# Keys in runs of 64 KB: one key buffer and two value buffers in the place of a ring of three

## The chip, the core and the metric

The kernel runs on one core of one Trainium2 chip. The metric is the device time of an execution in microseconds: the median of three runs before the change is 189.44 us (189.35 to 189.58). Beside it stands one profiled execution; its span of 187.4 us is the time inside the program that the trace shows. "Same" means within 2%.

## What is computed

One decoding step of a transformer block in its parallel form, for two sequences (B = 2) with one new token each. The normalized row goes through attention over the last W = 4096 positions of a cache and through a dense layer with the mish activation; both are added to the input.

```python
def reference(A_x, A_k_cache, A_v_cache, A_wq, A_wo, B_x, B_w1, B_b1, B_w2):
    # A_x: 2 x 1 x 448; caches: 2 x 8 heads x 32768 x 256; 16 query heads of 256, all bf16
    xn = _layernorm(A_x)
    # attention, W = 4096
    q = (xn @ wq)                             # 16 heads; two of them share a key/value head
    k, v = k_cache[:, :, Sk - W:], v_cache[:, :, Sk - W:]
    scores = einsum("bhqd,bhkd->bhqk", q, k) * 256 ** -0.5
    o = einsum("bhqk,bhkd->bhqd", softmax(scores), v)
    attention = o @ wo
    # dense layer
    h = xn @ w1 + b1
    dense = (h * tanh(softplus(h))) @ w2
    return A_x + attention + dense            # B_x takes no part
```

(Shortened, with the same names.) The keys that are read have 2 x 8 x 4096 x 256 x 2 B = 33.6 MB, the values as much; with the weights wq, wo, w1 and w2 the kernel reads 77.67 MB for each step and computes little with every byte.

## The kernel before

The 16 pairs of sequence and key head are worked through in U = 4 units of J = 4 pairs. The keys of one unit are 8 MiB: each of the 128 partitions takes 128 positions of one pair, 64 KB that lie together in the cache. SBUF is shared out in pools. Keys, values, wq, w1 and w2 go through one ring of three buffers of 32 KB for each partition, so a unit's keys come in two transfers of 4 MiB whose runs are 32 KB long, and its values in two of 4 MiB.

```python
kv_pool = ctx.enter_context(tc.tile_pool(name="kv", bufs=3))
kt_pool = ctx.enter_context(tc.tile_pool(name="kt", bufs=1))
wo_pool = ctx.enter_context(tc.tile_pool(name="wo", bufs=2))
...
KE = T * Dh                                   # 32 * 256; RK = 2

def ring(name):
    return kv_pool.tile([P, RK * KE], BF16, tag="kv", name=name)

def load_k(u, r):
    t = ring("k")
    src = kview[u][:, s0:, :].rearrange("j (c t) d -> c j (t d)", c=C)
    nc.sync.dma_start(out=t[:], in_=src[:, :, r * RK * KE : (r + 1) * RK * KE])
    k_t[u, r] = t

def load_v(u, g, lo=0, hi=TV):
    if lo == 0:
        v_t[u, g] = ring("v")
    ...
```

The waits follow from the buffers: a transfer into a buffer of the ring is issued when the last reader of what the buffer held is done. All the large transfers are issued in program order from the sync queue.

For the scores the keys must lie with the head dimension on the partitions. VectorE transposes them in blocks of 32 x 32, as pairs of bf16 in one fp32, two instructions for each half of a unit's keys; the result of each half has a tile of its own (32 KB for each partition, `kt0` and `kt1`). TensorE multiplies them with the query, ScalarE takes the exponential, VectorE transposes the weights back, and TensorE multiplies them with the values.

```python
kt = [kt_pool.tile([P, T * NB, RK, P // (R * J), J], FP32, name=f"kt{i}") for i in range(NH)]

def turns(u, i):
    t = k_t.pop((u, i))
    for r in range(RK):
        nc.vector.transpose(out=kt[i][:, :, r, :, :], in_=...)      # 128 x 4096 fp32

def scores(u, i):                              # cut
    ...                                        # mask: one matmul with ident
    for n in range(NB):
        for e in range(2):
            for w in range(4):                 # 4 * 2 * 4 = 32 matmuls
                nc.tensor.matmul(sc[32 * w : 32 * (w + 1)]...,
                    lhsT=qd[:, u, 2 * n + e, :, :]..., rhs=ktm[i][:, n, e, :, 16 * w : 16 * (w + 1)], ...)
    nc.scalar.activation(out=ex[:, :, :, i, :], in_=sc[:], func=ACT.Exp, scale=scale)
    if i == NH - 1:
        ...                                    # VectorE: ex transposed to the weights p, swap
```

`weigh` sums the weights, `values` multiplies them with the values, `gather` and `finish` make the unit's output, `relay` and `mix_early` multiply it with wo. The program order, which each engine follows for its own instructions:

```python
load_w1()
turns(0, 0); project(); scores(0, 0); turns(0, 1); dense_in(); mish(); scores(0, 1); weigh(0)
for u in range(U - 1):
    load_k(u + 1, 0); load_v(u, 0); load_k(u + 1, 1); load_v(u, 1); load_wo(u)
    turns(u + 1, 0)
    values(u, 0)
    scores(u + 1, 0)
    turns(u + 1, 1)
    values(u, 1)
    gather(u); finish(u)
    scores(u + 1, 1)
    relay(u); mix_early(u)
    if u < U - 2:
        weigh(u + 1)
u = U - 1
load_v(u, 0); load_v(u, 1, 0, 32); load_wo(u); load_v(u, 1, 32, 56); load_v(u, 1, 56, TV)
for part in range(len(w2_parts)):
    load_w2(part)                              # four transfers, into a buffer of the ring
carry(); values(u, 0); values(u, 1, 32); weigh(u); gather(u, last=False)
values_fixed(u, 1, 32, 56); values_fixed(u, 1, 56, TV); finish(u)
mix(u)                                         # wo of the last unit
for part in range(len(w2_parts)):
    dense_out(part)                            # w2; then the result is stored
```

(Several calls are put on one line here.)

Of the kernel before, what the change touches and what calls it, by code (L numbers as in the profile page):

```python
# [11 lines left out]
BF16 = mybir.dt.bfloat16  # L12
FP32 = mybir.dt.float32
# [4 lines left out]
def kernel(  # L18
# [13 lines left out]
    nc = tc.nc  # L32
    P = 128
    G = 4
    J = 4
    R = 4
    RK = 2

    Bsz, Sq, D = A_x.shape
# [11 lines left out]
    T = CT // R  # L51
# [17 lines left out]

    lead_pool = ctx.enter_context(tc.tile_pool(name="lead", bufs=1))  # L70
    lead_pool.tile([P, 192], BF16, name="lead")
    kv_pool = ctx.enter_context(tc.tile_pool(name="kv", bufs=3))
    kt_pool = ctx.enter_context(tc.tile_pool(name="kt", bufs=1))
    wo_pool = ctx.enter_context(tc.tile_pool(name="wo", bufs=2))
    p_pool = ctx.enter_context(tc.tile_pool(name="pp", bufs=1))
    consts = ctx.enter_context(tc.tile_pool(name="consts", bufs=1))
# [11 lines left out]
    vview = A_v_cache.rearrange("b (k u) s d -> u (b k) s d", u=U)  # L88

    def ring(name):  # L90
        return kv_pool.tile([P, RK * KE], BF16, tag="kv", name=name)

    k_t, v_t, wo_t = {}, {}, {}

    def load_k(u, r):
        t = ring("k")
        src = kview[u][:, s0:, :].rearrange("j (c t) d -> c j (t d)", c=C)
        nc.sync.dma_start(out=t[:], in_=src[:, :, r * RK * KE : (r + 1) * RK * KE])  # L98
        k_t[u, r] = t

    def load_v(u, g, lo=0, hi=TV):
        if lo == 0:
            v_t[u, g] = ring("v")
        t = v_t[u, g]
        src = vview[u][:, s0:, :].rearrange("j (g x t) d -> g x j (t d)", g=GV, x=C)
        nc.sync.dma_start(
            out=t[:, lo * Dh : hi * Dh], in_=src[g, :, :, lo * Dh : hi * Dh]
        )
# [15 lines left out]

    x_bf = consts.tile([Bsz, D], BF16)
    nc.scalar.dma_start(out=x_bf[:, :], in_=A_x.flatten_outer_dims())
    b1_sb = consts.tile([2, F2], BF16)
    nc.scalar.dma_start(out=b1_sb[:], in_=B_b1.rearrange("(k f) -> k f", k=2))

    load_k(0, 0)  # L130
    wq = ring("wq")
    nc.sync.dma_start(  # L132
        out=wq[:, 0 : NS * HW], in_=A_wq.flatten().rearrange("(p e) -> p e", p=P)
    )
    wq_t = [wq[:, i * HW : (i + 1) * HW] for i in range(NS)]
    load_k(0, 1)

    ident = consts.tile([P, P], BF16)
    make_identity(nc, ident[:])
# [12 lines left out]
    for k in range(KU):  # L152
# [14 lines left out]
        out=rstd[:], in_=mv[:, 1:2], func=ACT.Sqrt, bias=eps_t[:], scale=1.0  # L167
    )
    nc.vector.reciprocal(out=rstd[:], in_=rstd[:])
    xn_bf = consts.tile([Bsz, D], BF16)  # L170
    nc.vector.tensor_scalar(
        out=xn_bf[:],
        in0=x_bf[:],
        scalar1=mv[:, 0:1],
        scalar2=rstd[:],
# [31 lines left out]
                )  # L207

    xr_ps = ps_m.tile([P, NS, Bsz], BF16, tag="m", name="xr_ps")
    xn_v = xn_bf[:].rearrange("b (a k) -> b a k", k=NS)  # L210
    for s in range(NS):
        r = s // 2
        step = 3 + s % 2
# [39 lines left out]
    def add_rows(lhsT, rows, stop=False):  # L253
# [7 lines left out]
                skip_group_check=True,  # L261
            )

    kt = [
        kt_pool.tile([P, T * NB, RK, P // (R * J), J], FP32, name=f"kt{i}") for i in range(NH)
    ]
    ktm = [
        kt[i][:].bitcast(BF16).rearrange("p (t n) r c (j e) -> p n e t (r c j)", n=NB, e=2)
        for i in range(NH)
    ]  # L270

    def turns(u, i):
        t = k_t.pop((u, i))
        for r in range(RK):
            nc.vector.transpose(  # L275
                out=kt[i][:, :, r, :, :],
                in_=t[:, r * KE : (r + 1) * KE].bitcast(FP32).rearrange(
                    "p (a c j) -> p a c j", c=P // (R * J), j=J
                ),
            )  # L280

    spread = {}
    for n in range(2):
        for e in range(2):
            o = n * 64 + e
            sp = consts.tile([P, G, 32], BF16, name=f"sp{n}{e}")
            nc.gpsimd.tensor_copy(
                out=sp[:],
                in_=ident[:, o : o + 63 : 2].unsqueeze(1).to_broadcast([P, G, 32]),
            )  # L290
            spread[n, e] = sp

    def project():
        q_ps = ps_m.tile([P, 512], FP32, tag="m", name="q_ps")
        for s in range(NS):
            for u in range(U):
                nc.tensor.matmul(  # L297
                    q_ps[32 * u : 32 * (u + 1), :],
                    lhsT=xs[:, s, :],
                    rhs=wq_t[s][:, u * 512 : (u + 1) * 512],  # L300
                    start=(s == 0),
                    stop=(s == NS - 1),
                    skip_group_check=True,
                )
        q_sb = small.tile([P, 4, P], BF16, tag="vs", name="q_sb", bufs=1)
        nc.scalar.copy(out=q_sb[:].rearrange("p a m -> p (a m)"), in_=q_ps[:])
        qt_ps = ps_m.tile([P, 4, P], BF16, tag="m", name="qt_ps")
        for a in range(4):
            nc.tensor.transpose(qt_ps[:, a, :], q_sb[:, a, :], ident[:])  # L309
        qT = consts.tile([P, 2, U, Bsz, KU, rep], BF16)  # L310
        q_v = qt_ps[:].rearrange("p (h c) (u r) -> p c u r h", c=2, u=U)
        for c in range(2):
            for b in range(Bsz):
                nc.vector.tensor_copy(  # L314
                    out=qT[:, c, :, b, :, :], in_=q_v[:, c, :, b : KU * Bsz : Bsz, :]
                )
        qr_ps = ps_m.tile([P, 2 * NB, U, NQ], FP32, tag="m", name="qr_ps")
        for n in range(NB):
            for e in range(2):
                nc.tensor.matmul(  # L320
                    qr_ps[:, 2 * n + e, :, :].rearrange("p u q -> p (u q)"),
                    lhsT=spread[n % 2, e][:].rearrange("p g a -> p (g a)"),
                    rhs=qT[:, n // 2].rearrange("p u b k h -> p (u b k h)"),
                    start=True,
                    stop=True,
                    skip_group_check=True,
                )
        for g in range(G):
            rows = slice(g * 32, (g + 1) * 32)
            nc.vector.tensor_copy(  # L330
                out=qd[rows, :, :, g, :],
                in_=qr_ps[rows].rearrange("p n u q -> p u n q"),
            )
# [12 lines left out]
    def scores(u, i):  # L346
        if i == 0:
            state["ex"] = small.tile([P, T, 4, NH, J], BF16, tag="ex", name="ex", bufs=1)
        ex = state["ex"]
        sc = ps_sc.tile([P, T, 4, J], FP32, tag="sc", name="sc")  # L350
        nc.tensor.matmul(  # L351
            sc[:].rearrange("p t c m -> p (t c m)"),
            lhsT=ident[:],
            rhs=mneg[:].rearrange("p a j -> p (a j)"),
            start=True,
            stop=False,
            skip_group_check=True,
        )
        for n in range(NB):
            for e in range(2):  # L360
                for w in range(4):
                    nc.tensor.matmul(  # L362
                        sc[32 * w : 32 * (w + 1)].rearrange("p t c m -> p t (c m)"),
                        lhsT=qd[:, u, 2 * n + e, :, :].rearrange("p g q -> p (g q)"),
                        rhs=ktm[i][:, n, e, :, 16 * w : 16 * (w + 1)],
                        start=False,
                        stop=(n == NB - 1 and e == 1),
                        skip_group_check=True,
                    )
        nc.scalar.activation(out=ex[:, :, :, i, :], in_=sc[:], func=ACT.Exp, scale=scale)  # L370
        if i == NH - 1:
            for h in range(NH):
                nc.vector.transpose(  # L373
                    out=p_all[:, :, h * TH : (h + 1) * TH, :].rearrange("p g t q -> p t g q"),
                    in_=ex[:, h * TH : (h + 1) * TH].rearrange(
                        "p t c i m -> p t (c i m)"
                    ).rearrange("p t (g q) -> p t g q", g=G),
                )
            swap()
# [124 lines left out]
    def load_w1():  # L504
        t = ring("w1")
        nc.sync.dma_start(
            out=t[:, 0 : NS * F2], in_=B_w1.flatten().rearrange("(p e) -> p e", p=P)
        )
        state["w1"] = t
# [44 lines left out]

    def load_w2(part):
        if part == 0:
            state["w2"] = ring("w2")
        k, lo, hi = w2_parts[part]
        w2_in = B_w2.flatten().rearrange("(k p e) -> k p e", k=2, p=P)
        at = k * KH  # L560
        nc.sync.dma_start(  # L561
            out=state["w2"][:, at + lo * D : at + hi * D],
            in_=w2_in[k, :, lo * D : hi * D],
        )
# [7 lines left out]
            )  # L572

    load_w1()
    turns(0, 0)
    project()
    scores(0, 0)
# [2 lines left out]
    mish()  # L580
    scores(0, 1)
    weigh(0)
    for u in range(U - 1):
        load_k(u + 1, 0)
        load_v(u, 0)
        load_k(u + 1, 1)
        load_v(u, 1)
        load_wo(u)
        turns(u + 1, 0)
        values(u, 0)  # L590
        scores(u + 1, 0)
        turns(u + 1, 1)
        values(u, 1)
        gather(u)
        finish(u)
        scores(u + 1, 1)
        relay(u)
        mix_early(u)
        if u < U - 2:
            weigh(u + 1)  # L600
    u = U - 1
    load_v(u, 0)
    load_v(u, 1, 0, 32)
    load_wo(u)
    load_v(u, 1, 32, 56)
# [54 lines left out]
```

## Time and profile before

| what | value |
|---|---|
| time, median of 3 runs | 189.44 us |
| span of the profiled execution | 187.4 us |
| read from HBM | 77.67 MB, 414 GB/s over the span |
| VectorE busy | 92.9 us (50%) |
| of it the 16 transposes of keys | 70.1 us, 4417 ns each |
| TensorE busy, matmuls | 78.0 us (42%) |
| ScalarE busy | 12.4 us (7%) |
| GpSimd busy | 4.7 us (2%) |
| mean granted TensorE clock | 0.727 |

How to read it: busy time is the sum of an engine's instructions, and engines work beside each other, so the shares do not add up to 100%. The page cuts the span into 40 slices of 187.4 / 40 = 4.7 us and gives each a digit, the busy share in tenths; 9 is 90% or more. Transfers are counted apart, by queue and by packet. A line of a timeline has the start, the busy time, the engine, the line of the kernel, the operation with its operands and shapes, and in brackets how long the engine had stood idle before and what ended that. Lines are numbered by the kernel before: L275 is the transpose of keys, L362 the scores, L408 the values, L441 the last values, L255 the last products with wo and w2. "Landing" of a transfer is when the one who waits for it goes on.

### The profile page before, as it was taken

What the parts mean: (1) busy time and instruction counts of PE and PEld (TensorE: products, weight loads), DVE (VectorE), ACT (ScalarE), POOL (GpSimd) and SP (SyncE); (2) the same over time, 40 slices, a digit from 0 to 9 for tenths busy, and PEclk for the clock granted to TensorE, in tenths of its full rate; (3) what the DMA queues carried; (4) which work ended last, traced back from release to release, by engine and by line L of the source; (5) the groups of instructions that cost most, each with busy time, mean ns of one, the idle gap of its engine ahead of it and who ended that gap; (6) DMA issues with size and microseconds to landing.
All of it is one profiled execution on the core that took longest, in us unless ns stands there. A gap on an engine that the chain in (4) does not pass through costs nothing.

```text
span 187.4 us, 1956 instructions
## 1 busy us (share of the span) xinstructions
PE 78.0 (42%) x856; PEld 34.9 (19%) x856; DVE 92.9 (50%) x93; ACT 12.4 (7%) x26; POOL 4.7 (2%) x16
## 2 busy tenths in 40 slices
PE   0300277594119200882049002870067005854963
PEld 0100122361003100340013001430022002422552
DVE  6709814983793098038940395048910592040101
ACT  3000030101000100110000100110001000120101
POOL 8100000000000000000000000000000000000000
PEclk9999999957555855699555755798557655999555
DMA  6999999999999999999999999999999999999991
GB/s 211 448 421 410 456 420 413 461 444 448 441 406 406 437 442 393 467 441 448 448 420 395 434 434 429 438 437 448 448 434 406 420 441 420 441 416 397 434 405 49
DMA packets 4451, 77.78 MB, mean 415 GB/s; under 512 B 470, under 2 KB 1244, under 8 KB 2012
## 3 DMA queue, kind: packets, MB, share of 16 engines
q1 hardware_dynamic: 4436, 77.66, 96.9%
q8 instruction: 6, 0.10, 0.2%
q10 hardware_dynamic: 8, 0.01, 0.0%
q14 instruction: 1, 0.01, 0.0%
HBM read 77.67 MB, written 0.00 MB: 414 GB/s over the span
## 4 chain that ended last, share of the span: by engine, by line
DMA 79%; DVE 12%; PE 4%; issue 3%; SPq 1%; DVEq 0%
DMA k<-in_A_k_cache_dram 44%; DMA v<-in_A_v_cache_dram 23%; DMA w<-in_B_w_dram 12%; DVE kt L275 12%; PE pv L408 4%; PE acc L255 1%; SPq L98 0%; SPq L132 0%; SPq L561 0%; DVEq L655 0%; DVE res L626 0%; DVE t_sb L541 0%
## 5 line engine op out<-in xcount | busy, mean ns | idle before, releaser
L275 DVE STREAM_TRANSPOSE kt<-k 128x4096 f32<-128x4096 f32 x16 | 70.1, 4417 | 36.0 <-DMA k<-in_A_k_cache_dram 36.0
L408 PE MATMUL pv<-v,p 128*32 128x512 bf16 x240 | 25.0, 589 | 70.1 <-DMA v<-in_A_v_cache_dram 70.1
L408 PEld LDWEIGHTS <-p 128*32 128x32 bf16 x240 | 8.9, 131 | 83.5 <-issue 60.3
L362 PE MATMUL sc<-kt,qd 128*32 128x512 bf16 x256 | 21.5, 482 | 1.4 <-DVE qd L330 1.4
L453 DVE TENSOR_TENSOR oT<-o,rec 128x16 bf16<-128x16 f32 x4 | 0.7, 174 | 23.1 <-PE o L426 18.9
L373 DVE STREAM_TRANSPOSE p<-ex 128x512 bf16<-128x512 bf16 x8 | 5.2, 690 | 10.8 <-ACT ex L370 10.8
L370 ACT ACTIVATE ex<-sc 128x512 bf16<-128x512 f32 x8 | 4.8, 597 | 77.7 <-PE sc L362 77.7
L362 PEld LDWEIGHTS <-qd 128*32 128x32 bf16 x256 | 7.3, 112 | 13.8 <-issue 9.1
L297 PE MATMUL q_ps<-wq,xs 128*32 128x512 bf16 x28 | 3.2, 629 | 13.8 <-DMA wq<-in_A_wq_dram 13.8
L394 DVE TENSOR_REDUCE rec<-dn 128x8 f32<-128x512 f32 x4 | 2.8, 691 | 11.2 <-PE dn L386 11.2
L426 PE MATMUL o<-sel,vs 128*128 128x8 f32 x32 | 5.2, 289 | 2.1 <-ACT vs L420 2.1
L420 ACT COPY vs<-pv 128x512 f32<-128x512 f32 x4 | 2.3, 586 | 54.3 <-PE pv L408 54.3
L487 PE MATMUL early<-wo,ox 128*2 128x448 bf16 x24 | 5.0, 352 | 1.9 <-ACT ox L478 1.9
L426 PEld LDWEIGHTS o<-sel,vs 128*128 128x128 f32 x32 | 4.8, 228 | 5.3 <-ACT vs L420 5.3
L525 PE MATMUL h_ps<-xs,w 128*128 128x4 bf16 x49 | 3.7, 196 | 2.3 <-DMA w<-in_B_w_dram 2.3
L386 PE MATMUL dn<-p,ones 128*128 128x512 bf16 x8 | 3.0, 466 | 3.8 <-DVE p L344 3.8
L351 PE MATMUL sc<-mneg,ident 128*128 128x512 bf16 x8 | 4.1, 516 | 0.0
L218 PE MATMUL xr_ps<-ident,xrows 2*128 2x2 bf16 x7 | 1.0, 182 | 7.1 <-DVE xrows L217 7.1
L297 PEld LDWEIGHTS <-xs 128*32 128x32 bf16 x28 | 1.1, 136 | 15.4 <-issue 15.4
L525 PEld LDWEIGHTS <-w 128*128 128x128 bf16 x49 | 3.2, 149 | 2.5 <-DMA w<-in_B_w_dram 2.4
L145 DVE COPY halves<-ident 2x4 bf16<-2x4 bf16 x1 | 1.9, 1914 | 1.3 <-POOL ident masks.py:199 1.3
L314 DVE COPY qT<-qt_ps 128x16 bf16<-128x16 bf16 x4 | 0.4, 166 | 4.3 <-PE qt_ps L309 4.3
(67 smaller groups left out, 45.8 us busy)
## 6 DMA issues: line engine op xcount, KB each, us to landing
k<-in_A_k_cache_dram SPq DMA_DIRECT2D x8, 4096.0 KB, 27.5
v<-in_A_v_cache_dram SPq DMA_DIRECT2D x7, 4096.0 KB, 21.2
wq<-in_A_wq_dram SPq DMA_DIRECT2D x1, 3584.0 KB, 20.8
wo<-in_A_wo_dram SPq DMA_DIRECT2D x3, 896.0 KB, 21.5
v<-in_A_v_cache_dram SPq DMA_DIRECT2D x1, 2048.0 KB, 17.5
w<-in_B_w_dram SPq DMA_DIRECT2D x1, 1568.0 KB, 13.0
v<-in_A_v_cache_dram SPq DMA_DIRECT2D x1, 1536.0 KB, 21.7
wo<-in_A_wo_dram SPq DMA_DIRECT2D x2, 448.0 KB
```

The source lines that it names most:

```text
L275: nc.vector.transpose(out=kt[i][:, :, r, :, :], in_=t[:, r * KE : (r + 1) * KE].bitcast(FP32).rearrange("p (a c j) -> p a c j", c=P // (R ...
L297: nc.tensor.matmul(q_ps[32 * u : 32 * (u + 1), :], lhsT=xs[:, s, :], rhs=wq_t[s][:, u * 512 : (u + 1) * 512], start=(s == 0), stop=(s == N ...
L351: nc.tensor.matmul(sc[:].rearrange("p t c m -> p (t c m)"), lhsT=ident[:], rhs=mneg[:].rearrange("p a j -> p (a j)"), start=True, stop=Fal ...
L362: nc.tensor.matmul(sc[32 * w : 32 * (w + 1)].rearrange("p t c m -> p t (c m)"), lhsT=qd[:, u, 2 * n + e, :, :].rearrange("p g q -> p (g q) ...
L370: nc.scalar.activation(out=ex[:, :, :, i, :], in_=sc[:], func=ACT.Exp, scale=scale)
L373: nc.vector.transpose(out=p_all[:, :, h * TH : (h + 1) * TH, :].rearrange("p g t q -> p t g q"), in_=ex[:, h * TH : (h + 1) * TH].rearrang ...
L386: nc.tensor.matmul(dn[:].rearrange("p a q -> p (a q)"), lhsT=ones[:], rhs=p_run[:, i].rearrange("p t q -> p (t q)"), start=(i == 0), stop= ...
L394: nc.vector.tensor_reduce(out=rec[:], in_=dn[:].rearrange("p a q -> p q a"), axis=AXIS.X, op=ALU.add)
L408: nc.tensor.matmul(pv[32 * w : 32 * (w + 1), :, :].rearrange("p x d -> p (x d)"), lhsT=p_run[:, g, 4 * a : 4 * a + 4, :].rearrange("p t q ...
L426: nc.tensor.matmul(po[:, c, :], lhsT=sb[:, x, c::2], rhs=sel[:, x, :], start=(x == 0 and c == 0), stop=(last and x == 1), skip_group_check ...
L487: nc.tensor.matmul(early[:], lhsT=ox[:, i, :], rhs=w[:, i, :], start=False, stop=(u == U - 2 and i == 7),)
L525: nc.tensor.matmul(h_ps[:, i, :, :].rearrange("p k b -> p (k b)"), lhsT=w1_v[:, s, i, :], rhs=xs[:, s, 0 : 2 * Bsz], start=False, stop=(s ...
```

## The change

The keys of units 1 to 3 are each loaded in one transfer of 8 MiB, so that a partition's 64 KB come in one run of consecutive bytes. For that the ring of three is split: one key buffer of 64 KB for each partition and two value buffers of 32 KB, which wq and w1 use first (w2 takes the key buffer at the end). Unit 0 keeps its two transfers, with wq between them, into the two halves of the key buffer. The SBUF that this takes is won back in two places: the transposed keys go through a ring of three pieces of 16 KB (each the result of one transpose) in the place of two tiles of 32 KB, and the biases b1, the normalized row and the four spread matrices lie in the first buffer of the wo pool, which wo takes over later. The biases are loaded in four transfers in the place of one. The order of the loads and of `values` changes with the buffers: the first values of a unit are loaded ahead of the next unit's keys and used right after the weights are made. The arithmetic is the same.

Its purpose is that the keys, 33.6 MB of the 77.67, come in fewer and longer runs.

The diff, cut to its core (left out: the renaming that follows from `first`):

```diff
--- before.py
+++ after.py
@@ -69,8 +69,9 @@
 
     lead_pool = ctx.enter_context(tc.tile_pool(name="lead", bufs=1))
     lead_pool.tile([P, 192], BF16, name="lead")
-    kv_pool = ctx.enter_context(tc.tile_pool(name="kv", bufs=3))
-    kt_pool = ctx.enter_context(tc.tile_pool(name="kt", bufs=1))
+    k_pool = ctx.enter_context(tc.tile_pool(name="kk", bufs=1))
+    v_pool = ctx.enter_context(tc.tile_pool(name="vv", bufs=2))
+    kt_pool = ctx.enter_context(tc.tile_pool(name="kt", bufs=3))
     wo_pool = ctx.enter_context(tc.tile_pool(name="wo", bufs=2))
     p_pool = ctx.enter_context(tc.tile_pool(name="pp", bufs=1))
     consts = ctx.enter_context(tc.tile_pool(name="consts", bufs=1))
@@ -88,15 +89,16 @@
     vview = A_v_cache.rearrange("b (k u) s d -> u (b k) s d", u=U)
 
     def ring(name):
-        return kv_pool.tile([P, RK * KE], BF16, tag="kv", name=name)
+        return v_pool.tile([P, TV * Dh], BF16, tag="v", name=name)
 
     k_t, v_t, wo_t = {}, {}, {}
 
-    def load_k(u, r):
-        t = ring("k")
+    def load_k(u, lo=0, hi=NH):
+        if lo == 0:
+            k_t[u] = k_pool.tile([P, NH * RK * KE], BF16, tag="k", name="k")
         src = kview[u][:, s0:, :].rearrange("j (c t) d -> c j (t d)", c=C)
-        nc.sync.dma_start(out=t[:], in_=src[:, :, r * RK * KE : (r + 1) * RK * KE])
-        k_t[u, r] = t
+        cols = slice(lo * RK * KE, hi * RK * KE)
+        nc.sync.dma_start(out=k_t[u][:, cols], in_=src[:, :, cols])
 
     def load_v(u, g, lo=0, hi=TV):
         if lo == 0:
@@ -124,16 +126,19 @@
 
     x_bf = consts.tile([Bsz, D], BF16)
     nc.scalar.dma_start(out=x_bf[:, :], in_=A_x.flatten_outer_dims())
-    b1_sb = consts.tile([2, F2], BF16)
-    nc.scalar.dma_start(out=b1_sb[:], in_=B_b1.rearrange("(k f) -> k f", k=2))
-
-    load_k(0, 0)
+    first = wo_pool.tile([P, KU * rep * 2 * D], BF16, tag="wo", name="first")
+    b1_sb = first[0:2, 0:F2]
+    for c in range(0, F2, F2 // 4):
+        cols = slice(c, c + F2 // 4)
+        nc.scalar.dma_start(out=b1_sb[:, cols], in_=B_b1.rearrange("(k f) -> k f", k=2)[:, cols])
+
+    load_k(0, 0, 1)
     wq = ring("wq")
     nc.sync.dma_start(
         out=wq[:, 0 : NS * HW], in_=A_wq.flatten().rearrange("(p e) -> p e", p=P)
     )
     wq_t = [wq[:, i * HW : (i + 1) * HW] for i in range(NS)]
-    load_k(0, 1)
+    load_k(0, 1, NH)
 
     ident = consts.tile([P, P], BF16)
     make_identity(nc, ident[:])
@@ -261,31 +266,28 @@
                 skip_group_check=True,
             )
 
-    kt = [
-        kt_pool.tile([P, T * NB, RK, P // (R * J), J], FP32, name=f"kt{i}") for i in range(NH)
-    ]
-    ktm = [
-        kt[i][:].bitcast(BF16).rearrange("p (t n) r c (j e) -> p n e t (r c j)", n=NB, e=2)
-        for i in range(NH)
-    ]
+    kt = {}
 
     def turns(u, i):
-        t = k_t.pop((u, i))
         for r in range(RK):
+            t = kt_pool.tile([P, T * NB, P // (R * J), J], FP32, tag="kt", name="kt")
+            at = (i * RK + r) * KE
             nc.vector.transpose(
-                out=kt[i][:, :, r, :, :],
-                in_=t[:, r * KE : (r + 1) * KE].bitcast(FP32).rearrange(
+                out=t[:],
+                in_=k_t[u][:, at : at + KE].bitcast(FP32).rearrange(
                     "p (a c j) -> p a c j", c=P // (R * J), j=J
                 ),
             )
+            kt[r] = t[:].bitcast(BF16).rearrange("p (t n) c (j e) -> p n e t (c j)", n=NB, e=2)
 
     spread = {}
     for n in range(2):
         for e in range(2):
             o = n * 64 + e
-            sp = consts.tile([P, G, 32], BF16, name=f"sp{n}{e}")
+            at = F2 + D + (2 * n + e) * P
+            sp = first[:, at : at + P].rearrange("p (g a) -> p g a", g=G)
             nc.gpsimd.tensor_copy(
-                out=sp[:],
+                out=sp,
                 in_=ident[:, o : o + 63 : 2].unsqueeze(1).to_broadcast([P, G, 32]),
             )
             spread[n, e] = sp
@@ -362,7 +364,7 @@
                     nc.tensor.matmul(
                         sc[32 * w : 32 * (w + 1)].rearrange("p t c m -> p t (c m)"),
                         lhsT=qd[:, u, 2 * n + e, :, :].rearrange("p g q -> p (g q)"),
-                        rhs=ktm[i][:, n, e, :, 16 * w : 16 * (w + 1)],
+                        rhs=kt[w // 2][:, n, e, :, 16 * (w % 2) : 16 * (w % 2 + 1)],
                         start=False,
                         stop=(n == NB - 1 and e == 1),
                         skip_group_check=True,
@@ -554,7 +556,7 @@
 
     def load_w2(part):
         if part == 0:
-            state["w2"] = ring("w2")
+            state["w2"] = k_pool.tile([P, NH * RK * KE], BF16, tag="k", name="w2")
         k, lo, hi = w2_parts[part]
         w2_in = B_w2.flatten().rearrange("(k p e) -> k p e", k=2, p=P)
         at = k * KH
@@ -572,6 +574,7 @@
             )
 
     load_w1()
+    load_v(0, 0)
     turns(0, 0)
     project()
     scores(0, 0)
@@ -580,14 +583,13 @@
     mish()
     scores(0, 1)
     weigh(0)
+    values(0, 0)
     for u in range(U - 1):
-        load_k(u + 1, 0)
-        load_v(u, 0)
-        load_k(u + 1, 1)
+        load_k(u + 1)
         load_v(u, 1)
         load_wo(u)
+        load_v(u + 1, 0)
         turns(u + 1, 0)
-        values(u, 0)
         scores(u + 1, 0)
         turns(u + 1, 1)
         values(u, 1)
@@ -598,8 +600,8 @@
         mix_early(u)
         if u < U - 2:
             weigh(u + 1)
+            values(u + 1, 0)
     u = U - 1
-    load_v(u, 0)
     load_v(u, 1, 0, 32)
     load_wo(u)
     load_v(u, 1, 32, 56)
```

More of the change, by code (lines that the diff above doesn't have):

```diff
@@ L169 @@
     nc.vector.reciprocal(out=rstd[:], in_=rstd[:])
-    xn_bf = consts.tile([Bsz, D], BF16)
+    xn_bf = first[0:Bsz, F2 : F2 + D]
     nc.vector.tensor_scalar(
-        out=xn_bf[:],
+        out=xn_bf,
         in0=x_bf[:],
@@ L209 @@
     xr_ps = ps_m.tile([P, NS, Bsz], BF16, tag="m", name="xr_ps")
-    xn_v = xn_bf[:].rearrange("b (a k) -> b a k", k=NS)
+    xn_v = xn_bf.rearrange("b (a k) -> b a k", k=NS)
     for s in range(NS):
@@ L321, in project @@
                     qr_ps[:, 2 * n + e, :, :].rearrange("p u q -> p (u q)"),
-                    lhsT=spread[n % 2, e][:].rearrange("p g a -> p (g a)"),
+                    lhsT=spread[n % 2, e].rearrange("p g a -> p (g a)"),
                     rhs=qT[:, n // 2].rearrange("p u b k h -> p (u b k h)"),
```

## The prediction, before the result was known

> **What bounds the kernel now.** I read the page from the slices and the DMA queues down, since an engine that is half idle cannot carry the time. The page's section of slices first:
>
> ```profile
> DMA  6999999999999999999999999999999999999991
> GB/s 211 448 421 410 456 420 413 461 444 448 441 406 406 437 442 393 467 441 448 448 420 395 434 434 429 438 437 448 448 434 406 420 441 420 441 416 397 434 405 49
> ```
>
> In 38 of 40 slices the 16 DMA engines are busy for 90% or more. Then the queue, from the page, and the shares of the chain that ended last:
>
> ```profile
> q1 hardware_dynamic: 4436, 77.66, 96.9%
> ...
> DMA 79%; DVE 12%; PE 4%; issue 3%; SPq 1%; DVEq 0%
> ```
>
> The loads take 0.969 x 187.4 = 181.6 us of packet time out of a span of 187.4. The other 5.8 us are the start (the first issue stands at 0.73, the packet records begin at 2.15 us) and the tail after the last weights land (183.6 us in the chain). The 12% of VectorE in the chain is no second bound: there the chain steps from one load to a buffer that a transpose frees, while other loads fill the DMA engines. How regular the stream is can be read from what TensorE waits for in its timeline:
>
> ```profile
> 74.97 3.52 PE L408 MATMUL pv<-v,p 128*32 128x512 bf16 x32 [12.66 <-DMA v<-in_A_v_cache_dram]
> ...
> 96.42 3.61 PE L408 MATMUL pv<-v,p 128*32 128x512 bf16 x32 [10.44 <-DMA v<-in_A_v_cache_dram]
> ...
> 115.80 3.59 PE L408 MATMUL pv<-v,p 128*32 128x512 bf16 x32 [12.57 <-DMA v<-in_A_v_cache_dram]
> ```
>
> and from VectorE's timeline, where a second half of the keys is awaited:
>
> ```profile
> 65.28 8.77 DVE L275 STREAM_TRANSPOSE kt<-k 128x4096 f32<-128x4096 f32 x2 [7.58 <-DMA k<-in_A_k_cache_dram]
> ...
> 106.11 8.77 DVE L275 STREAM_TRANSPOSE kt<-k 128x4096 f32<-128x4096 f32 x2 [10.53 <-DMA k<-in_A_k_cache_dram]
> ...
> 147.18 8.77 DVE L275 STREAM_TRANSPOSE kt<-k 128x4096 f32<-128x4096 f32 x2 [10.40 <-DMA k<-in_A_k_cache_dram]
> ```
>
> Keys at 65.28, values at 74.97: 9.69 us for 4 MiB. Values at 96.42, keys at 106.11: 9.69. Keys at 106.11, values at 115.80: 9.69. That is 4,194,304 B / 9.69 us = 433 GB/s with nothing between transfers. One unit (two halves of keys, two of values, 0.9 MB of wo) passes in 106.11 - 65.28 = 40.8 us. The reader should see in these lines that every engine waits for data and data waits for no engine.
>
> **What the Trainium skill says.** "DMA: Bandwidth & Descriptors", section Bandwidth, gives 435 GB/s for the 16 ports on the SBUF side; the 433 above is that rate, so there is hardly a better one to be had. The same page, Why small descriptors are slow, puts a fixed cost on each packet and says that joining packets is worth it only for very small ones. The packet records agree: the median is 1,213 ns for 32,768 B and 611 ns for 16,384 B, so the second 16 KB cost 602 ns and a fixed 9 ns remains. "SBUF — State Buffer", The DMA setup-cost knee, speaks of about 2 us for every transfer; the even 9.69 us show that here it lies under the transfer ahead. The same page, Who interferes with whom, says that a DMA does not contend with a compute engine; the 16 transposes take 4,393 to 4,446 ns each beside a full stream, so I let none grow.
>
> **The change part by part.**
>
> *Runs of 64 KB.* Same bytes. In units 1 to 3 the 256 runs of 32 KB become 128 of 64 KB: 3 x 128 = 384 fewer, 24 on each of 16 engines, at 9 ns: 24 x 9 = 0.2 us saved, if a run is one packet. Three issues of 0.54 us less on the sync queue save nothing, since they lie beside the stream.
>
> *One key buffer.* Now the keys of unit u+1 may be issued only when the last of four transposes of unit u is done. Unit 1's keys land, whole, when their second half did before, at 65.3: the same transfers stand ahead (the first values moved in front of them). Four transposes are 4 x 4.385 (half of the 8.77 shown) = 17.5 us, so the issue comes at 82.8. From issue to first packet I take 1.4 us, the 0.73 to 2.15 of the start: 84.2. What lies in the queue behind unit 1's keys is 4 MiB of values, wo and 4 MiB of values; the last of it lands 9.7 us before 96.42, at 86.7, and its packets end about 0.5 us earlier, at 86.2. **Margin about 2 us**; by the packet records the quickest DMA engine is 1.4 us ahead of the slowest and has 0.5 us. A short idling of the quickest costs nothing, since the slowest ends the load. For unit 1 itself: the transposes end at 40.7 (31.93 + 8.77), first packet at 42.1, and the stream is filled to about 45. Unit 3 repeats unit 2, 40.8 us later. So no idle time on the path: 0.
>
> *Three half pieces for transposed keys.* In units 1 to 3 the fourth transpose must wait for the first scores, which read the piece it overwrites. These can start when two pieces are done, at 65.3 + 8.8 = 74.1, and the row of scores has taken 2.7 to 4.1 us (2.67 in unit 1, at a granted clock of 0.6): done by 77 to 78.5. The fourth transpose is due at 65.3 + 13.2 = 78.5. It just fits; at the worst 0.2 us late, within the margin.
>
> *Two value buffers.* The first values of a unit are now used right after its weights are made, some 30 us before the next load of that buffer enters the stream. Second values: used 9.7 us after their keys land plus 3.6 us of matmuls, in time again. w1 no longer waits for a transpose (before it was issued at 22.6), but its turn in the queue is unchanged. 0.
>
> *Biases, normalized row and spreads in a wo buffer; biases in four transfers.* Three more issues of 0.24 us on ScalarE's queue move the row work by some 0.7 to 2 us; it ended at 8.9 (the last xs at 8.26 + 0.61) and is needed at 22.4. 0.
>
> *The tail.* This moves most. Before, only two transposes remained at 147.18, and VectorE was done at 155.95. Now four remain: 147.2 + 17.5 = 164.7. The last scores then end about 1.9 us later at 166.7 (32 matmuls took 1.91), the weights are ready 2.95 us after that, as before (164.28 to 167.23): 169.65 instead of 167.23. TensorE's end in the timeline before shows what takes up these 2.4 us:
>
> ```profile
> 168.77 1.91 PE L408 MATMUL pv<-v,p 128*32 128x512 bf16 x32 [0.85 <-DMA v<-in_A_v_cache_dram]
> 173.54 1.64 PE L408 MATMUL pv<-v,p 128*32 128x512 bf16 x16 [2.86 <-DMA v<-in_A_v_cache_dram]
> ...
> 179.43 1.87 PE L441 MATMUL o<-p,v 128*128 128x8 bf16 x64 [1.65 <-DMA v<-in_A_v_cache_dram]
> 181.56 0.92 PE L255 MATMUL acc<-wo,oT 128*2 128x112 bf16 x32 [0.27 <-DVE oT L453]
> 182.55 0.82 PE L255 MATMUL acc<-w,act_bf 128*2 128x112 bf16 x28
> 183.67 1.09 PE L255 MATMUL acc<-w,act_bf 128*2 128x112 bf16 x28 [0.30 <-DMA w<-in_B_w_dram]
> ```
>
> Values of unit 3 start at 169.7 to 170.7 and last 1.9 us (3.6 at the low clock): done by 171.6 to 174.3, while the next load lands at 173.5. Of a delay of at most 0.8 the wait of 1.65 us before 179.43 takes the rest. So the end still waits for the last w2, at 183.6. 0. The w2 loads need the key buffer at 164.7, and the stream reaches them after 179. 0.
>
> *Sum*: -0.2 + 0 = -0.2 us; I give 0.1 back for the thin margins. 189.44 - 0.1 = **189.3 us**.
>
> **Rivals.** *(a) VectorE becomes the bound through the single buffer.* For it: the margin is 2 us of a 40.8 us cycle, and the fourth transpose waits on scores. Were the fourth transpose a whole 4.4 us late, 2.4 us of the margin would be lost at units 2 and 3: about +4.8 us, 194. Against it: TensorE was idle for 12.7 us before the values at 74.97, so the scores start on time. *(b) TensorE's tail becomes the bound.* For it: 2.4 us of delay against waits of 0.85, 2.86, 1.65 and 0.30. Against it: those sum to 5.7. At the low clock throughout perhaps +0.5 us, 190. *(c) Long runs move faster than the packet records say*, through the memory's side. For it: only that the stream's rate in the slices varies, 393 to 467; but that is how whole packets fall into slices, and keys and values, with different strides, take the same 9.69 us. If a port could do 1% better on half the bytes, -0.9 us, 188.5. *(d) Runs of 64 KB move worse*, being cut or not overlapping their successor. No row speaks for or against it, since no such run is in this kernel; a gap of 50 ns per run would add 24 x 0.05 = 1.2 us.
>
> **Range and chances.** The stream's floor does not move, (a) in part, (b) and (d) would add up to a microsecond or so, (c) would take less than one. So 188.6 to 190.3 for 8 in 10. Faster by over 2% would need 185.7, less than the packets' 181.6 plus the 5.8 at both ends: 0.02. Slower by over 2% (193.2) needs (a) in full or a bad (d): 0.05. Within 2%: 0.93.
>
> **What would show it.** Right: DMA still at 9 in the slices, packet time still about 181.5 us; keys landing at about 65, 106 and 147 us; four transposes in a row of 17.5 us; keys issued at 82.8 and 123.6; the last w2 landing near 183.5. Wrong: slices of DMA under 9 near 86 and 127 us (a); an idle time before the last matmuls that ends with VectorE or TensorE instead of w2 (b); packets of 64 KB that take less or more than 2,417 ns (c, d). Wrong as a whole would be a span away from 187.4 by over 1 us, which only idle DMA engines or another packet rate could make.

## The result and the profile after

The changed kernel takes 191.92 us (median of 6 runs, 191.16 to 192.57) against 189.39 us before: the ratio is 1.0129, interval 1.0103 to 1.0156. By the 2% line that is "same", but it is 2.5 us slower, clear of the scatter of the runs, and outside the range of the prediction (188.6 to 190.3).

The page after, its slices (190.4 / 40 = 4.76 us each), its queue of loads, and the shares of the chain that ended last:

```profile
DMA  6999998999999799998999999999998999999990
GB/s 221 434 420 440 455 434 376 457 410 537 441 441 441 337 441 412 433 475 317 430 441 441 392 434 420 441 475 403 441 441 365 420 401 466 434 396 395 394 379 14
...
q1 hardware_dynamic: 4004, 77.66, 96.1%
...
DMA 64%; DVE 21%; issue 7%; PE 4%; SPq 2%; DVEq 0%
```

The loads took 0.961 x 190.4 = 183.0 us of packet time instead of 181.6, for the same bytes: packets have become slower, and beside that a DMA engine is on average without a packet for 1.6 us more of the span (7.4 instead of 5.8). The slices have to be read with care: packets of 64 KB are put into slices whole, so the 7 at 62 to 67 us stands for no pause, and the slice near 86 us (the 8 with 317 GB/s) says something only together with the packet records; the one near 127 us shows 9. VectorE's share of the chain has risen from 12% to 21%: the chain now steps through all four transposes of a unit before each load of keys.

VectorE's timeline after (start, busy time, line, operation, and how long it had waited for what), the three lines that answer to those at 65.28, 106.11 and 147.18 before:

```profile
65.36 17.42 DVE L275 STREAM_TRANSPOSE kt<-k 128x4096 f32<-128x4096 f32 x4 [16.53 <-DMA k<-in_A_k_cache_dram]
...
107.58 17.42 DVE L275 STREAM_TRANSPOSE kt<-k 128x4096 f32<-128x4096 f32 x4 [18.19 <-DMA k<-in_A_k_cache_dram]
...
149.95 17.42 DVE L275 STREAM_TRANSPOSE kt<-k 128x4096 f32<-128x4096 f32 x4 [18.36 <-DMA k<-in_A_k_cache_dram]
```

Up to the keys of unit 1 the two kernels are level. From unit 1 to unit 2 it takes 42.22 us, from 2 to 3 42.37; before it took 40.83 and 41.07. **The whole loss, 1.4 + 1.3, lies in these two turns**, and the tail hands it on nearly unchanged: the last matmuls, which started at 183.67 before, start at 186.57, 2.9 us later, and still wait for w2.

```profile
186.57 1.13 PE L260 MATMUL acc<-w,act_bf 128*2 128x112 bf16 x28 [0.26 <-DMA w<-in_B_w_dram]
```

Where in the turn? The sync queue's timeline shows the issue of unit 2's keys, a hundredth from the predicted 82.8:

```profile
82.81 0.54 SPq L101 DMA_DIRECT2D k<-in_A_k_cache_dram  x1
83.44 0.56 SPq L108 DMA_DIRECT2D v<-in_A_v_cache_dram  x1
84.05 0.59 SPq L115 DMA_DIRECT2D wo<-in_A_wo_dram  x1
```

The packet records of the trace show more. A transfer of keys is cut into 128 packets of 64 KB, 8 for each of the 16 DMA engines. The first key packet starts at 84.95, at the moment when its engine finishes the values ahead, and most engines follow on without a pause. But the packets are slow. A packet of 64 KB takes 2,418 ns in a quiet stretch; of those that start from 84.95 to 89.13 us, 25 take 67 to 1,623 ns longer. Below, a packet that takes over 60 ns more than the median of its size is called slow, and what it takes more its excess. Between 80 and 100 us the excess is 0.92 us per engine. And not every engine finds its keys waiting: the records don't name the engine of a packet, but at 85.75 us only 13 are under way, and the three engines without one begin at 85.97, 86.50 and 87.06, that is 3.2 to 4.3 us after the issue. Idle time adds 0.27 us per engine.

It is not the mean that sets the loss, but the engine that ends last. The one that began its keys at 86.50 had been idle until then and had 1.45 us of excess; with 8 x 2.418 us this gives 107.3, where the last key packet ends. The engine that came last from the values, at 86.59, would undisturbed have ended at 86.59 + 8 x 2.418 = 105.9. The difference, 1.3, is nearly the whole loss of the turn.

At the next load of keys (issued 125.03, first packet 126.73) it is the same again: 22 slow packets between 122 and 140 us, 0.46 us of excess and 0.24 of idle time, and one engine that began at 128.83 with 1.42 us of excess ends the load. The keys of unit 1, also in runs of 64 KB, had no slow packet between 44 and 64 us.

### The profile page after: what moved, and what is told of

Its sections match the earlier page's. It is cut to its first block, busy times and chain, and to the rows that moved or that the text cites. A ratio compares the mean times of both kernels' runs of the same rounds, so it can differ in the third digit from the quotient of the medians.

```text
span 190.4 us, 1950 instructions
## 1 busy us (share of the span) xinstructions
PE 73.2 (38%) x852; PEld 35.1 (18%) x856; DVE 92.5 (49%) x93; ACT 12.4 (7%) x26; POOL 4.7 (2%) x16
## 3 DMA queue, kind: packets, MB, share of 16 engines
HBM read 77.67 MB, written 0.00 MB: 408 GB/s over the span
## 4 chain that ended last, share of the span: by engine, by line
DMA 64%; DVE 21%; issue 7%; PE 4%; SPq 2%; DVEq 0%
DMA k<-in_A_k_cache_dram 55%; DVE kt L275 21%; DMA w<-in_B_w_dram 10%; PE sc L364 2%; PE pv L410 1%; SPq L108 1%; PE acc L260 1%; SPq L121 1%; SPq L101 0%; SPq L563 0%; SPq L137 0%; DVEq L657 0%; DVE res L628 0%; DVE oT L455 0%; DVE t_sb L543 0%
## 5 line engine op out<-in xcount | busy, mean ns | idle before, releaser
L364 PE MATMUL sc<-kt,qd 128*32 128x512 bf16 x256 | 27.1, 533 | 75.9 <-DVE kt L275 72.8
L364 PEld LDWEIGHTS <-qd 128*32 128x32 bf16 x256 | 9.8, 118 | 89.5 <-issue 86.0
L410 PE MATMUL pv<-v,p 128*32 128x512 bf16 x240 | 18.9, 450 | 1.8 <-DMA v<-in_A_v_cache_dram 1.5
L410 PEld LDWEIGHTS <-p 128*32 128x32 bf16 x240 | 7.9, 115 | 12.1 <-issue 9.0
L428 PE MATMUL o<-sel,vs 128*128 128x8 f32 x32 | 4.4, 265 | 2.2 <-ACT vs L422 2.2
L428 PEld LDWEIGHTS o<-sel,vs 128*128 128x128 f32 x32 | 4.1, 196 | 4.2 <-ACT vs L422 4.2
L388 PE MATMUL dn<-p,ones 128*128 128x512 bf16 x5 | 2.0, 447 | 4.0 <-DVE p L346 3.8
L443 PE MATMUL o<-p,v 128*128 128x8 bf16 x64 | 1.9, 168 | 3.1 <-DMA v<-in_A_v_cache_dram 3.1
L353 PE MATMUL sc<-mneg,ident 128*128 128x512 bf16 x7 | 2.9, 412 | 0.0
```

Of the source, the lines that this page charges most:

```text
L353: nc.tensor.matmul(sc[:].rearrange("p t c m -> p (t c m)"), lhsT=ident[:], rhs=mneg[:].rearrange("p a j -> p (a j)"), start=True, stop=Fal ...
L364: nc.tensor.matmul(sc[32 * w : 32 * (w + 1)].rearrange("p t c m -> p t (c m)"), lhsT=qd[:, u, 2 * n + e, :, :].rearrange("p g q -> p (g q) ...
L410: nc.tensor.matmul(pv[32 * w : 32 * (w + 1), :, :].rearrange("p x d -> p (x d)"), lhsT=p_run[:, g, 4 * a : 4 * a + 4, :].rearrange("p t q ...
L428: nc.tensor.matmul(po[:, c, :], lhsT=sb[:, x, c::2], rhs=sel[:, x, :], start=(x == 0 and c == 0), stop=(last and x == 1), skip_group_check ...
```

## The experiments

**The theories.** L: the keys of units 2 and 3 are issued too late, because one buffer has to be transposed whole before. R: runs of 64 KB move worse. O: something else in the change. Later, within L: L1, it is enough that a transfer is there when the queue runs out; L2, it must be there some microseconds ahead; L3, the three transfers issued in a row hold each other up. Each experiment changes the changed kernel, and its edit is shown cut to the core; all were timed against the kernel before on the same chip, whose median was between 189.34 and 189.45 us.

**e1, late halves: runs of 32 KB, issued as late.**

```diff
-        load_k(u + 1)
+        load_k(u + 1, 1, 2)      # second half first: both issued after the last transpose
+        load_k(u + 1, 0, 1)
```

> The changed kernel, but the keys of units 1 to 3 come in two transfers with runs of 32 KB, second half first, both issued after the last transpose of the unit before, so that the keys are whole at the same time as in the changed kernel. Theory L (the keys are issued too late, some DMA engines run dry and the restart costs): nothing changes, 191.9 us within 0.5, keys of unit 2 complete at about 107.5 and of unit 3 at 150. Theory R (runs of 64 KB move worse than runs of 32 KB): back to 189.4. Theory O (biases in parts, order of the loads, pieces of transposed keys): 191.9.

192.69 us, ratio 1.0178 (1.0161 to 1.0195). The loss stays without a single run of 64 KB among the keys; R falls. It is even 0.8 us above the changed kernel, more than the 0.5 that the expectation allowed, and what the extra comes from is not shown. Keys whole at 107.73 and 149.44, 26 slow packets between 80 and 100 us.

**e2, early halves: the same buffers, but the first half first.** Both halves are issued as soon as the buffer is free; since the first two transposes run while the second half is on its way, that is at 74.03:

```profile
74.03 1.18 SPq L101 DMA_DIRECT2D k<-in_A_k_cache_dram  x2
```

```diff
-        load_k(u + 1)
+        load_k(u + 1, 0, 1)
+        load_k(u + 1, 1, 2)
```

> The changed kernel with the same buffers, order of loads and pieces, but the keys of units 1 to 3 in two transfers with runs of 32 KB, first half first. The first two transposes then run while the second half is on its way, the last transpose ends some 8.8 us after the keys are whole and not 17.4, and the next keys can be issued 8.7 us sooner (74 instead of 82.8). Theory L: no engine runs dry, 189.4 us within 0.4. Theory R: 189.4 too. Theory O: still about 191.9.

189.72 us, ratio 1.0019 (1.0012 to 1.0027). The loss is gone but for 0.3 us; O falls for all but that. One slow packet between 80 and 100 us.

**e3, one transpose less: runs of 64 KB, issued early.** In units 1 and 2 the last quarter of the keys is not transposed; its scores use an older piece.

```diff
         for r in range(RK):
+            if u in (1, 2) and (i, r) == (1, 1):
+                continue
```

> The changed kernel with its runs of 64 KB, but without the last of the four transposes in units 1 and 2 (the scores of that quarter use the piece before, so the result is another); the key buffer is free 4.4 us sooner, at 78.4 for unit 2. Theory L: the queue holds out, no slow packets near 85 and 127, keys complete at about 106 and 147, time 189.2 (189.4 less 0.2 for 384 packets fewer). Theory R: 191.9, the packets of 64 KB being what they were. Theory O: 191.9.

189.39 us, ratio 0.9998 (0.9989 to 1.0007). VectorE's timeline and the issue of unit 2's keys:

```profile
65.41 13.10 DVE L277 STREAM_TRANSPOSE kt<-k 128x4096 f32<-128x4096 f32 x3 [17.29 <-DMA k<-in_A_k_cache_dram]
...
106.26 13.10 DVE L277 STREAM_TRANSPOSE kt<-k 128x4096 f32<-128x4096 f32 x3 [17.11 <-DMA k<-in_A_k_cache_dram]
...
147.30 17.42 DVE L277 STREAM_TRANSPOSE kt<-k 128x4096 f32<-128x4096 f32 x4 [17.23 <-DMA k<-in_A_k_cache_dram]
```

```profile
78.53 0.54 SPq L101 DMA_DIRECT2D k<-in_A_k_cache_dram  x1
```

Keys at 106.26 and 147.30, as before the change, and runs of 64 KB without loss. The same six microseconds in the stretches of both kernels show it directly. The last column is what the DMA engines moved in GB/s; each packet is counted whole, so a single stretch is rough. First the changed kernel, from 84 to 90 us:

```profile
84.00:86.00 2.00, 1.37 (x24) 0.65 (x17) 0.50 (x1) 0.81 (x3) 0.00 (x0) 1.00 1.41 508
86.00:88.00 2.00, 1.60 (x9) 0.55 (x8) 1.67 (x5) 0.00 (x0) 0.00 (x0) 1.00 1.03 360
88.00:90.00 2.00, 1.85 (x33) 0.77 (x32) 0.89 (x2) 0.00 (x0) 0.00 (x0) 1.00 0.54 229
```

Then e3:

```profile
84.00:86.00 2.00, 1.36 (x23) 0.57 (x16) 0.74 (x2) 0.81 (x3) 0.00 (x0) 1.00 1.33 573
86.00:88.00 2.00, 1.60 (x9) 0.45 (x6) 1.42 (x4) 0.00 (x0) 0.00 (x0) 1.00 1.13 492
88.00:90.00 2.00, 2.00 (x34) 0.81 (x33) 0.90 (x2) 0.00 (x0) 0.00 (x0) 1.00 0.98 426
```

TensorE, VectorE and ScalarE do nearly the same work in both; only the DMA engines move less, although 8 MiB of keys have been issued.

**e4, one transpose more, in unit 1 alone.**

```diff
+            if u == 1 and (i, r) == (1, 1):
+                nc.vector.transpose(out=t[:], in_=...)      # the same once more
```

> The changed kernel with the last transpose of unit 1 alone done twice, so that the keys of unit 2 are issued 4.4 us later, at 87.2. Theory L: the stream is short of the whole 4.4 us once, 191.9 + 4.4 = 196.3, keys of unit 2 complete at 112 and of unit 3 at 154.3. Theory R or O: VectorE is half idle, so 191.9 to 192.3.

194.14 us, ratio 1.0247 (1.0232 to 1.0262): slower, but by 4.7 us and not by 6.9. Both key issues and what VectorE saw:

```profile
87.50 0.53 SPq L101 DMA_DIRECT2D k<-in_A_k_cache_dram  x1
...
128.55 0.54 SPq L101 DMA_DIRECT2D k<-in_A_k_cache_dram  x1
```

```profile
65.56 17.43 DVE L275 STREAM_TRANSPOSE kt<-k 128x4096 f32<-128x4096 f32 x4 [17.09 <-DMA k<-in_A_k_cache_dram]
...
111.10 17.42 DVE L275 STREAM_TRANSPOSE kt<-k 128x4096 f32<-128x4096 f32 x4 [15.41 <-DMA k<-in_A_k_cache_dram]
...
152.06 17.42 DVE L275 STREAM_TRANSPOSE kt<-k 128x4096 f32<-128x4096 f32 x4 [16.95 <-DMA k<-in_A_k_cache_dram]
```

Here the queue does run dry: the first key packet starts at 88.83, 1.33 us after the issue. The engines stand idle for 3.7 us on average, and their first packets are slow by 0.96 us per engine; together 4.7, and the turn of 111.10 - 65.56 = 45.54 us is 4.7 too long. The next turn, 40.96 us, has no loss at all. So the size was wrong in two places: of the 4.7 us by which the issue is later than in the changed kernel (87.50 against 82.81) only 3.7 are dry time, because in the changed kernel the keys came before the queue ran out, and the second loss, 1.3 us there, did not come. Yet its lead was as short as before (128.55 to a first packet at 130.29) and 12 packets were slow. By the records they fell on engines that were ahead: the engine that came last from the values, at 132.16, was not touched and ended at 151.48, and none ended later than 151.56. So a short lead does not cost every time; it depends on which engine is hit.

**e5 and e6, three quarters and half of the last transpose, in units 1 and 2.** The rest of the piece is set to zero.

```diff
+            a = 96 if u in (1, 2) and (i, r) == (1, 1) else T * NB     # 64 in e6
+            if a < T * NB:
+                nc.gpsimd.memset(t[:, a:], 0.0)
             nc.vector.transpose(
-                out=t[:],
-                in_=...
+                out=t[:, 0:a],
+                in_=...[:, 0:a]
```

> The changed kernel, but the last of the four transposes in units 1 and 2 does three quarters of its columns (the rest of the piece is set to zero on GpSimd, so the result is another): the key buffer is free 1.1 us sooner, keys of unit 2 issued at about 81.7 instead of 82.8, some 3.2 us before the first DMA engine comes to them (84.9 in the kernel with one transpose less). Theory L1 (a transfer has only to be there when the queue runs out, 1.4 us after its issue): no loss, 189.4. Theory L2 (a DMA engine must have the next transfer some microseconds ahead, or its first packets are slow): part of the loss, 190.0 to 191.5, with slow packets left near 85 and 127.

> As before with half of the columns of the last transpose in units 1 and 2: keys of unit 2 issued at about 80.6, 4.3 us before the first DMA engine comes to them. Theory L1: 189.4. Theory L2: little or no loss left, 189.4 to 190.3, in any case less than with three quarters.

189.96 us, ratio 1.0029 (1.0016 to 1.0042), and 189.37 us, ratio 0.9997 (0.9988 to 1.0006). L1 falls, L2 stands. The profile of e5 is its slowest run (191.44; its runs go from 189.38 to 191.44), with 14 slow packets between 80 and 100 us; e6 has one. VectorE's timeline in e5:

```profile
65.59 16.36 DVE L278 STREAM_TRANSPOSE kt<-k 128x4096 f32<-128x4096 f32 x4 [17.29 <-DMA k<-in_A_k_cache_dram]
...
107.83 16.36 DVE L278 STREAM_TRANSPOSE kt<-k 128x4096 f32<-128x4096 f32 x4 [19.24 <-DMA k<-in_A_k_cache_dram]
...
148.87 17.42 DVE L278 STREAM_TRANSPOSE kt<-k 128x4096 f32<-128x4096 f32 x4 [18.10 <-DMA k<-in_A_k_cache_dram]
```

The first turn, with the lead of the table, takes 42.24 us and loses 1.4: one engine has 2.1 us of excess. The second takes 41.04 and loses nothing, with a lead of only 1.66 us and 28 slow packets: as in e4, the large excess fell on engines that were ahead.

With the changed kernel and e3 this makes a row, for unit 2's keys, with the lead as the time from the issue to the first key packet; the last line sets beside it the keys of unit 1 in the changed kernel:

| kernel | issued | first packet | lead, us | slow packets, 80 to 100 us | median time against before, us |
|---|---|---|---|---|---|
| changed | 82.81 | 84.95 | 2.14 | 26 | +2.5 |
| e5 | 81.97 | 84.94 | 2.97 | 14 | +0.5 (this run +2.0) |
| e6 | 80.72 | 84.83 | 4.11 | 1 | -0.1 |
| e3 | 78.53 | 84.86 | 6.33 | 1 | 0.0 |
| changed, unit 1's keys | 40.50 | 44.03 | 3.53 | 0 (44 to 64 us) | |

The first packets of unit 2's keys begin at nearly the same time in all four kernels. In e5, e6 and e3 no engine stood idle before its first key packet, so in e5 it was not enough that the packet was there; what differs in the row is how long the transfer had been issued. All profiled loads of 64 KB runs with full-sized packets ahead agree on the slow packets: nine with a lead of 1.3 to 3.0 us had 12 to 28, thirteen with 3.5 us or more had 0 to 6.

**e7, spaced: the transfers behind the keys issued 6 us later.**

```diff
             values(u + 1, 0)
+            v_t[u + 1, 1] = ring("v")
+            nc.vector.memset(v_t[u + 1, 1][:, 0:2], 0.0)      # its load waits for this
```

> The changed kernel with its whole arithmetic, but the second values and wo of units 1 and 2 are not issued right behind the keys (83.4 and 84.1 in the changed kernel): a small VectorE write into the value buffer at the end of the turn before holds them back to about 89.5, still long before the stream needs them. The keys are issued at 82.8 as in the changed kernel. Theory L3 (three transfers issued in a row hold up each other's start): the slow packets near 85 and 127 go, 189.4 to 190. Theory L1 or L2 (only the late issue of the keys counts): 191.9 within 0.6.

191.66 us, ratio 1.0112 (1.0086 to 1.0137). Unit 2's keys are issued at 82.65, the values behind them at 89.29, and 19 packets between 80 and 100 us are slow. L3 falls.

**e8, runs of 48 and 16 KB, the whole arithmetic.**

```diff
-            k_t[u] = k_pool.tile([P, NH * RK * KE], BF16, tag="k", name="k")
+            k_t[u] = (
+                k_pool.tile([P, 3 * KE], BF16, tag="k", name="k"),
+                k_pool.tile([P, KE], BF16, tag="kq", name="kq"),
+            )
         # two transfers, each issued when its own part has been transposed
```

> A version with the whole arithmetic: the key buffer in two parts, runs of 48 KB for the first three quarters of the keys and of 16 KB for the last, so that the keys of unit 2 are issued when three transposes are done, at about 73.5 instead of 82.8. All theories of a late issue: 189.4 to 189.8, no slow packets near 85 and 127. Theory O: 191.9.

189.71 us, ratio 1.0015 (1.0008 to 1.0022); keys issued at 73.43, one slow packet. It beats the changed kernel by 2.2 us and does not beat the kernel before. No run pointed to a version that beats both.

**e9, short packets ahead of the keys.**

```diff
-        load_v(u + 1, 0)
+        load_v(u + 1, 0, 0, 32)                   # for u < U - 2
+        for lo in range(32, TV, 8):
+            load_v(u + 1, 0, lo, lo + 8)          # runs of 4 KB
```

> The changed kernel with its whole arithmetic and its keys issued at 82.8, but of the first values of units 1 and 2, which lie right ahead of the next keys in the queue, the last 16 KB of each run come in four transfers with runs of 4 KB (159 ns each in the profile before) in the place of one run of 32 KB. Theory P (a DMA engine takes up the next one or two packets ahead of time, so the lead that the keys need is counted in packets): with packets of 0.16 us ahead a lead of 2 us is enough, 189.5 to 190.2, no slow packets near 85 and 127. Theory T (the lead is a time of some 3 to 4 us from issue to an undisturbed start under a full stream, whatever lies ahead): 191.9 within 0.7.

190.77 us, ratio 1.0069 (1.0054 to 1.0085): neither number. The key packets of unit 2 (from 85.66 us, a lead of 2.84) have no excess at all, but the short runs cost something themselves: 59 packets of 4 KB took some 0.1 us too long between 80.2 and 82.9 us. It leans to P; since the lead also grew by 0.7 us, it settles nothing. At unit 3's keys, with a lead of 2.22 us, 7 packets were slow.

**e10, half of the last transpose left out in unit 1 alone.** The edit of e6 with `u == 1`.

> Half of the last transpose left out in unit 1 alone (the rest of the piece set to zero, so the result is another): keys of unit 2 are issued at 80.6 as in the kernel that does so in both units, keys of unit 3 as late after their predecessors as in the changed kernel. If each late issue costs by itself: keys of unit 2 complete at 106.3, of unit 3 at about 148.4 instead of 147.1, time about 190.7, halfway between 189.4 and 191.9. If the second loss only follows from the disorder that the first leaves: 189.4 to 189.8.

190.23 us, ratio 1.0054 (1.0031 to 1.0078).

```profile
65.29 15.29 DVE L278 STREAM_TRANSPOSE kt<-k 128x4096 f32<-128x4096 f32 x4 [17.11 <-DMA k<-in_A_k_cache_dram]
106.10 17.42 DVE L278 STREAM_TRANSPOSE kt<-k 128x4096 f32<-128x4096 f32 x4 [17.68 <-DMA k<-in_A_k_cache_dram]
148.00 17.42 DVE L278 STREAM_TRANSPOSE kt<-k 128x4096 f32<-128x4096 f32 x4 [17.86 <-DMA k<-in_A_k_cache_dram]
```

The first turn takes 40.81 us, without loss; the second 41.90, 0.8 us more than before the change. The second loss does not need the first. The time is 0.9 us above the kernel before, between the 190.7 and the at most 189.8 that were expected of the two cases; the turns decide for the first case.

## Why the prediction was wrong

**The step that failed** is the one called "One key buffer", in its last sentence: "So no idle time on the path: 0". This term of the sum was mis-sized; it measures +2.5 to 2.8 us (1.4 and 1.3 in the two turns). Its times were right: keys at 65.36, four transposes of 17.42 us, the issue at 82.81, the quickest engine at the end of its values at about 84.9. What was wrong was the yardstick, "From issue to first packet I take 1.4 us". It came from the start of the kernel, where the queue is empty, and e4 gives 1.33 us for a queue that has run dry, so the number holds there for the first engine. Under a full stream it does not hold for every engine: three had their first packet only 3.2 to 4.3 us after the issue. And packets that are there in time can still be slow: in e5, at a lead of 3.0 us, no engine waited and 14 packets were slow; the keys of unit 1, at 3.5, had none. Measured by this, the margin of "about 2 us" was a shortfall of about 1 us. "A short idling of the quickest costs nothing, since the slowest ends the load" is right as a rule of counting, and e4's second turn shows it; but the quickest engine was only 1.6 us ahead of the slowest (84.95 against 86.59), and the one that began at 86.50 lost more than that by idling and slow packets together, so it became the slowest.

The Trainium skill's page "SBUF — State Buffer", The DMA setup-cost knee, on which the prediction leaned, was read too broadly. Its about 2 us for each transfer do lie under the transfer ahead, but only for one that is issued early enough, and in the kernel before every large transfer was: the shortest lead there, that of the first values of unit 0, is 4.0 us (issued at 39.88; by the packet records the first engine came to them at 43.9), and it left no slow packet. Here "early enough" lies between 3.0 and 3.5 us for packets of 32 KB ahead.

**What was right.** *Rival (a)*, the late issue through the single buffer, was named, but as idle time behind a fourth transpose that comes late; the fourth transpose came in time. *Rival (d)*, slow runs of 64 KB, did not come: e3 and e1 part the run's length from the lateness. *Runs of 64 KB* are one packet of 2,418 ns, 8 ns less than two of 32 KB; the 0.2 us expected of them are within the interval of e3 and e6 and not seen by themselves. *Three pieces for transposed keys*: the four transposes stand in one row of 17.42 us, without a pause for the scores. *Two value buffers, biases, spreads*: e2, which has them all, is within 0.3 us of the kernel before; the row work ended 0.4 us later. *The tail*: the last matmuls of the changed kernel wait 0.26 us for w2 where those before waited 0.30, so w2 still sets the end.

**What stays open.** Why a transfer with a lead of 2 to 3 us reaches some engines late, and why its first packets are slow even where no engine stands still: that an engine takes up coming packets ahead of time would fit the second, and e9 leans that way, but no run shows it alone. And the 0.3 us that e2 and e8 lie above the kernel before, with no slow packets to explain it.

## What to carry to other kernels

In a stream that fills the DMA engines, an issue is not safely in time when the queue still holds work, but when it holds several microseconds of it, here 3.5; count the lead from the issue to the end of what is queued, and compare it with a series of runs that vary the lead, not with the latency of an empty queue. A load is whole when its slowest engine is done, so look at that engine and not at the mean. Joining two buffers into one to get longer runs makes the release of the buffer later by all the work that used to overlap with the second half's arrival, here 8.8 us (82.81 against 74.03 in e2), while the longer runs brought no gain that the intervals show. If whole buffers must be kept, free them in parts (e2, e8): that took back 2.2 us of the 2.5.

## What the runs showed of the hardware

- A packet of 64 KB is possible and takes 2,418 ns (changed kernel); one of 32 KB takes 1,213.
- From the issue to the first packet of a dry queue it is 1.33 us in e4 (87.50 to 88.83) and 1.4 at the start of the kernel. "DMA: Bandwidth & Descriptors", Specifications, gives about 0.6 us to the first byte for transfers issued from the sync queue; measured is over twice that, from the start of the issue in the profile.
- The first packets after a dry queue are slow too: 0.96 us per engine in e4, 0.4 to 0.7 us at the start of every kernel here.
- Under a full stream, at a lead of 2.14 us, the first key packet of three engines came only 3.2 to 4.3 us after the issue; after the dry queue of e4 the last of the 16 came after 2.4 us (89.86 against 87.50).
- Unexpected was that at a lead of 2.97 us (e5) packets are slow, by up to 1.55 us, though every engine finds its first packet waiting.
